# Row sums moved off the early exponentials, and a new stored order, in an attention and gated-MLP kernel

## The chip, the cores and the metric

The kernel runs on one core of a Trainium2 chip. The metric is the device time of one execution in microseconds (us); smaller is better. The engines are TensorE (PE), VectorE (DVE), ScalarE (ACT), GpSimd (POOL) and SyncE (SP), whose queue issues the DMAs.

## The reference

Float32 throughout, with 8 batches of 576 positions, 8 heads of 64.

```
# attention, per batch and head (scale = 1/8)
q_d, k_d, v_d = means over 4 neighbouring positions          # 144 rows
out_up    = repeat(softmax(scale * q_d @ k_d.T) @ v_d, 4)    # pooled half
scores    = scale * q @ k.T, masked to |i - j| < 4
out_local = softmax(scores) @ v                              # local half
x = out_up + out_local                                       # (8, 576, 512)
# MLP with a spatial gate, per batch
h = gelu_tanh(x @ w_in);  u, v = halves of h                 # 512 columns each
v_n = (v - mean(v)) / sqrt(var(v) + 1e-6) * g_ln
v_s = w_sg @ v_n + b_sg
out = x + (u * v_s) @ w_out
```

## The kernel before

The work is cut into small named pieces. A number behind a name is the pair of heads `g` (32 of them: 8 batches of 4 pairs) or, with a dot, batch and tile of the MLP. An order written out by hand in the string `ORDER` says in which sequence the pieces are emitted and, behind a slash, on which engine; each engine runs its own pieces strictly in that sequence. Buffers (8 banks of PSUM `ps`, 10 of `X`, 38 of `R`) are handed out and taken back along the same order.

For one pair: `lq`, `lk`, `lv`, `lw` load q, k and two forms of v; `qs`, `ks`, `vs` sum four neighbours (on POOL two instructions each for q and k). `S` computes the local scores and `Y` the pooled ones (`YS` is both from pair 4 on). `mx`, `nx` and `my`, `ny` take row maxima and biases. `ea` (four) and `eb` (six) are the local exponentials, ten tiles of 64 columns, `ec` the three pooled ones. `re` adds the epsilon to the row sums, `rc` inverts them, `np` and `nq` scale. `T`, `U`, `t` turn the probabilities on PE, `pa`, `pb`, `pc`, `pe` copy them out of PSUM, and `D` multiplies by v. In pairs 0 to 3 `S` adds the mask on PE, and `D` sums v's four neighbours itself: 104 small matmuls. `oe`, `od`, `xa`, `xb` join both halves to x; `xh`, `xl`, `xc` split x into a high and a low part.

For the MLP, `v` (batch 0: `vk` by parts), `u`, `s`, `o` are the four products on PE, three matmuls with 32-bit operands for each product of the split parts. The pieces `w`, `wu`, `wq`, `wb`, `wt`, `wh`, `wl` with a letter `y`, `z` or `r` load a weight matrix and make its two parts; `wq0` to `wq4`, `whq`, `wlq` do so for `w_sg`.

Work that matters for the change: `exp(i)` writes each exponential with `accum_out`, so that ACT also delivers its row sum, which the profile shows as an extra ACTIVATION_READ_ACCUMULATOR. `dma` lets at most six loads be in flight: the seventh waits for the first (`DEPTH`). `lv` of pair g waits for `D` of pair g - 2 while g is below 6. `WARM` puts 28 and 20 matmuls on zeros ahead of `S0` and `S3`, wherever these stand in the order. Loads stand on SP's queue, except four of pairs 0 and 1, which are on ACT's.

Of the kernel before, what the change touches and what calls it, by code (L numbers as in the profile page):

```python
# [90 lines left out]
ea0 lq3 wuy3 qs0/P wly0/P wqy2/A S1 eb0 Y1 mx1 wby2 wuy2 wty3 wty2 Y0 my0 my1 nx1/A ny1/V wqy1/A wby1 ny0/A why3/V ec0
re0/V ec1 rc0 nq0/P wz2 lk3 wqz2/V lq2 S3 ea1 eb1 wbz2 wuz2 lk2 np0/P S2 mx3 ks2/V T0 wz3 wqz3/A qs2/P mx2 re1/A rc1
pa0/A wtz2 U0 lk4 t0 lv0/S qs3/V pb0/A pc0/A nx3/V pe0/V nx2/A lw0/S Y2 my2 ea2 eb2 ny2/A D0 wuy1 ks4/V wbz3 ec2 re2/A
lq4 qs4/V oe0/V od0 np1/P wz1 xa0 xb0 ks3/P nq1/P U1 wty1 rc2 np2/P T1 xh0/V wqz1/A nq2/P lv1/S pa1/V pb1/A pc1/A YS4
ma4 ea3 wz0 mb4 t1 pe1/V lq5 Y3 my3 xl0/P lv2 D1 eb3 wbz1 ny3/A ec3 oe1/A T2 U2 pa2/A pb2/A wqz0/A my4 vk3.0 ny4/A mx4
nx4/A od1 xa1 re3/A wly3/P t2 xb1 small lk5 qs5/P pc2/A rc3 vk1.0 xh1/V ec4 ks5/V lw2 pe2/A D2 nq3/P t3 np3/P why2/A
wbz0 eb4 oe2/V od2 xa2 xb2 T3 pa3/A U3 pb3/V pc3/V pe3/A YS5 my5 lk7 lv3 lw3 D3 wuz0 why1/A wly2/P lk6 ea4 wr0 wr1 ma5
mb5 mx5 xc0 wly1/V xl1/P vk2.0 vk2.1 re4/A rc4 nq4/V t4 ks6/V oe3/V ny5/A ec5 xh2/A xl2/V vk3.1 wuz3 wtz0 whz0/A xc1
wqr0/A nx5/A vk0.0 od3 xa3 xb3 whz2/V vk0.1 xh3/V wlz2/V wur0 wr3 wur3 np4/P xl3/V T4 U4 lv4 wtz3 wuz1 wqr3/A vk1.1
vk1.2 lw4 wq4 wbr0 pa4/A vk2.2 pb4/V wqr1/A wbr1 v0.2 ea5 wbr3 wtz1 ks7/V eb5 vk3.2 lq6 re5/V rc5 vk0.2 v0.0 pc4/A  # L100
pe4/V vs4 whz3/A qs6/V v0.1 vg0.1 v0.3 wtr0 wlz0/V wq2 wlz3/V vb0.1 vk4.0 vk4.1 vg0.2 vg0.0 D4 wur1 YS6 my6 vg0.3 wtr3
whz1/A lq8 vb0.0 xc2 wq0 lv5 vk4.2 nq5/P np5/V ma6 xc3 v0.4 wlz1/V mb6 whq2/A wtr1 ny6/A vb0.2 wq3 u0.3 vp0.0 vn0.0
wlq2/P ec6 vp0.2 mx6 lw5 vp0.1 u0.2 whq3/A wlq3/P va0.4/A vj0.4 wr2 wqr2/A lq7 vh0.0/A vb0.3 vg0.4 ua0.2 ua0.3 u0.4
ua0.4 u0.0 vn0.2 vh0.2/A u0.1 vn0.1 vh0.1/A vb0.4 wq1 whq1/A oe4/A vp0.3 whr3/A T5 vl0.2/V U5 t5 pa5/A u0.7 vn0.3
wlq1/V ua0.0 ua0.1 vl0.0/P vp0.4 u0.6 b vn0.4 vl0.1/V whq0/A wlq0/V whr1/A whq4/A wlq4/V vh0.3/A vl0.3/V vh0.4/A
vl0.4/V ua0.6 nx6/A u0.5 ua0.5 wlr1/V s0.1 sa0.1 wbr2 ea6 sm0.1/P whr0/A s0.3 sa0.3 qs7/V vs5 wlr3/P s0.0 sm0.3/V
sa0.0 sm0.0/V s0.2 eb6 re6/A wur2 wtr2 od4 qs8/V gh0.0/A rc6 nq6/P lk8 pb5/V pc5/V ua0.7 s0.4 sa0.2 np6/P sm0.2/V s0.5
sa0.5 gh0.1/A pe5/A s0.6 xa4 gl0.0/P whr2/A sa0.4 sm0.4/V sm0.5/V gh0.2/A sa0.6 sm0.6/P xb4 s0.7 U6 sa0.7 sm0.7/V
gh0.3/A gl0.3/P T6 pa6/A pb6/A pc6/A D5 oe5/A lw7 gl0.2/V gl0.1/V YS7 my7 od5 ks8/V xa5 xb5 t6 ma7 mb7 pe6/A lk9 lw6
xh4/A lv6 vs6 lq9 o0.7 ny7/A ec7 o0.6 mx7 oa0.6 wlr0/P D6 lv7 YS8 lw8 qs9/V oa0.7 o0.5 nx7/A ea7 lq10 my8 ma8 qs10/V  # L110
mb8 mx8 eb7 xl4/P xh5/V re7/A rc7 ny8/A nq7/V xl5/V wlr2/P o0.0 oe6/A od6 xa6 xb6 lk10 o0.1 ec8 nx8/A eb8 ea8 re8/A
o0.4 ks9/V oa0.4 xc5 t7 np7/P T7 oa0.0 oa0.5 vs7 U7 pa7/A pb7/V pc7/A xc4 rc8 oa0.1 np8/P o0.3 pe7/V D7 oe7/V xh6/A
YS9 lq11 nq8/P od7 xa7 xb7 xh7/A T8 ma9 my9 mb9 mx9 ny9/A ec9 U8 nx9/V ea9 t8 pa8/V pb8/V qs11/V ks10/V xl6/P pc8/A
pe8/V xl7/P os0.0 v1.0 vg1.0 vb1.0 v1.1 vg1.1 lv8 vs8 D8 oe8/A od8 YS10 my10 eb9 xa8 xb8 xc6 lv9 xc7 vb1.1 ma10 re9/V
v1.4 va1.4/A mb10 xh8/A vs9 vp1.1 vn1.1 v1.3 rc9 nq9/V lk12 vg1.3 v1.2 vp1.0 np9/P t9 T9 vj1.4 vn1.0 U9 o0.2 vg1.4 lw9
lk11 vg1.2 ks12/P pa9/A pb9/A pc9/A lq12 ks11/P ny10/A mx10 nx10/A ec10 vb1.3 vp1.3 vn1.3 vh1.3/A vl1.3/P pe9/V
vh1.1/V u1.2 vb1.2 vp1.2 ea10 oa0.2 oa0.3 D9 YS11 vb1.4 my11 vh1.0/V vl1.0/P eb10 ny11/V ma11 mb11 oe9/V re10/A u1.1
rc10 np10/V vl1.1/V nq10/P ec11 u1.4 ua1.4 ua1.2 u1.0 ua1.0 os0.3 vp1.4 ua1.1 mx11 vn1.2 vh1.2/V vl1.2/P T10 pa10/A
vn1.4 lv10 vh1.4/A vl1.4/V vs10 t10 U10 pb10/V u1.3 ua1.3 pc10/V pe10/A lq13 nx11/A ea11 s1.3 qs12/V eb11 xl8/V od9
xa9 s1.0 s1.1 sa1.1 sa1.0 sm1.1/V lk13 re11/A rc11 lw10 D10 YS12 oe10/A lv11 vs11 xb9 sa1.3 xh9/A np11/P sm1.0/P  # L120
nq11/P u1.6 lw11 lq14 qs13/P my12 ny12/A ma12 s1.2 mb12 mx12 ec12 nx12/V ea12 od10 xa10 s1.5 eb12 sa1.2 ua1.6 s1.4
xl9/P T11 xc8 os0.2 pa11/A sm1.3/V sm1.2/P gh1.1/A re12/V rc12 t11 np12/V sa1.5 nq12/P sa1.4 U11 pb11/V pc11/V u1.5
xb10 pe11/A ua1.5 sm1.5/P ks13/V t12 D11 YS13 lv12 oe11/A od11 xa11 lk15 xb11 ma13 T12 pa12/A U12 pb12/A xh10/A s1.6
mb13 pc12/V pe12/A my13 ny13/V ec13 mx13 nx13/V s1.7 lk14 ks14/V u1.7 xl10/V xh11/V xl11/V sm1.4/P v2.0 u2.6 ks15/P
eb13 vs12 qs14/P sa1.6 ea13 re13/V ua2.6 rc13 ua1.7 vg2.0 v2.3 os0.1 np13/P T13 pa13/A gh1.0/V gl1.0/P lw12 sm1.6/V
D12 lv13 oe12/A sa1.7 sm1.7/V gh1.3/V gl1.3/V gl1.1/V YS14 nq13/P U13 od12 xa12 gh1.2/A lw13 t13 vg2.3 vb2.0 xc11 ma14
mb14 gl1.2/P lq15 o1.4 my14 pb13/V xb12 ny14/V vs13 mx14 v2.1 ec14 lq16 o1.0 pc13/V nx14/A vp2.0 vn2.0 vh2.0/V pe13/V
D13 oa1.4 ea14 qs15/V eb14 oa1.0 YS15 my15 re14/V ny15/V ec15 ma15 mb15 mx15 rc14 v2.2 vg2.2 lk16 xc10 xc9 v2.4 lv14
vg2.1 vs14 np14/V vb2.1 T14 lw14 va2.4/A vj2.4 nx15/A nq14/P vl2.0/V oe13/A od13 xa13 xb13 ks16/P vp2.1 qs16/V vn2.1
# [885 lines left out]
```

## Time and profile before

| | us |
|---|---|
| three timed runs | 579.75, 578.34, 578.86 |
| median | 578.86 |
| span of the profiled execution | 578.3 |
| PE busy | 562.3 |
| DVE, ACT, POOL busy | 420.8, 355.8, 309.6 |

The profiled execution has no time of its own beside its span of 578.3 us, from first to last instruction; the timed runs lie 0 to 1.5 above it. A row of the timeline gives start, length, engine, line, operation, out<-in, and in brackets the idle time ahead of it with what ended it. Busy times of an engine overlap with those of others. "PEld" is PE's weight loading, which overlaps its matmuls.

### The profile page before, as it was taken

The page shows a single profiled execution, that of the slowest core. Times are in us where ns is not written, and L with a number is a line of the kernel's source. Part 1 is how long each engine was busy: PE and PEld are TensorE (multiplying, and loading weights), DVE is VectorE, ACT ScalarE, POOL GpSimd, SP SyncE. Part 2 cuts the span into 40 slices and gives each one's busy share as a digit, 9 for nine tenths or more (in the row PEclk, how much of TensorE's full clock was granted, in tenths as well). Part 3 has the DMA queues.
Part 4 walks back from the last instruction along what each step waited for, and adds up shares of the span by engine and source line. Part 5 has one row for each costly group of instructions (what it writes and reads, how often), then busy time and mean ns, then how long its engine had stood idle before and what let it go on. Part 6 is the DMA issues. An engine that isn't in the chain of part 4 may idle for free.

```text
span 578.3 us, 17588 instructions
## 1 busy us (share of the span) xinstructions
PE 562.3 (97%) x7040; PEld 524.0 (91%) x7040; DVE 420.8 (73%) x943; ACT 355.8 (62%) x1239; POOL 309.6 (54%) x391
## 2 busy tenths in 40 slices
...
GB/s 310 276 234 313 98 45 120 96 192 87 140 96 164 24 107 54 208 63 1 86 56 197 114 67 98 41 151 98 87 83 195 103 107 2 18 23 41 43 1 102
DMA packets 30609, 62.73 MB, mean 108 GB/s; under 512 B 3648, under 2 KB 3904, under 8 KB 30528
## 3 DMA queue, kind: packets, MB, share of 16 engines
...
q8 instruction: 55, 0.90, 0.7%
q10 hardware_dynamic: 576, 1.23, 0.6%
q14 instruction: 26, 0.21, 0.1%
...
## 4 chain that ended last, share of the span: by engine, by line
PE 91%; DVE 4%; DMA 2%; ACT 2%; issue 1%; ACTq 0%; DVEq 0%
PE ps L800 55%; PE ps L722 18%; PE ps L604 4%; PE ps L620 3%; PE ps L455 3%; PE ps L543 3%; PE ps L476 3%; PE ps L552 2%; DMA R<-in_qT_dram 1%; PE ps L955 1%; ACT L523 1%; ACT pd L523 1%; DVE stats L485 0%; PE ps L448 0%; DMA R<-in_v_dram 0%
## 5 line engine op out<-in xcount | busy, mean ns | idle before, releaser
L800 PE MATMUL ps<-wsg_h,R 128*128 128x288 f32 x576 | 120.5, 296 | 0.0
L800 PE MATMUL ps<-X,weight_z 128*128 128x288 f32 x512 | 109.4, 297 | 0.0
L800 PE MATMUL ps<-R,weight_r 128*128 128x288 f32 x768 | 108.4, 297 | 1.0 <-ACT R L734 0.8
L800 PEld LDWEIGHTS ps<-R,weight_r 128*128 128x128 f32 x768 | 103.1, 188 | 2.2 <-ACT R L734 0.9
L722 PE MATMUL ps<-weight_y,X 128*128 128x512 f32 x320 | 99.1, 404 | 0.0
L515 ACT ACTIVATE X<-X,nb 128x64 f32<-128x64 f32 x280 | 93.6, 339 | 2.8 <-DVE nb L494 2.3
L800 PEld LDWEIGHTS ps<-wsg_h,R 128*128 128x128 f32 x576 | 94.0, 188 | 0.2 <-DVE R L791 0.2
L800 PE MATMUL ps<-wsg_l,R 128*128 128x288 f32 x320 | 92.5, 295 | 0.0
L800 PEld LDWEIGHTS ps<-X,weight_z 128*128 128x128 f32 x512 | 84.3, 188 | 0.5
L800 PE MATMUL ps<-R,weight_z 128*128 128x288 f32 x256 | 75.5, 295 | 0.0
L722 PEld LDWEIGHTS ps<-weight_y,X 128*128 128x128 f32 x320 | 59.4, 191 | 12.5
L838 DVE SCALAR_TENSOR_TENSOR vs<-ps,g_sb,b_sb 128x288 f32<-128x288 f32 x64 | 32.7, 514 | 49.3 <-PE ps L800 43.9
L232 ACT CAST R<-R 128x512 fp32r<-128x512 f32 (+2 forms) x41 | 26.0, 645 | 62.4 <-DVE R L845 35.2
L800 PEld LDWEIGHTS ps<-wsg_l,R 128*128 128x128 f32 x320 | 60.3, 188 | 0.0
L763 POOL TENSOR_TENSOR rs<-rs,nhalf 128x1 f32<-128x1 f32 (+1 forms) x40 | 25.5, 641 | 64.9 <-DVE rs L754 60.9
L515 ACT ACTIVATION_READ_ACCUMULATOR X<-X,nb 128x1 f32 x280 | 53.5, 191 | 0.0
L722 PE MATMUL ps<-weight_y,R 128*128 128x512 f32 x128 | 51.2, 400 | 0.0
L439 POOL TENSOR_TENSOR pairs<-R 112x256 f32<-112x256 f32 x56 | 44.4, 793 | 9.2 <-DMA R<-in_v_dram 9.2
L845 POOL TENSOR_TENSOR R<-R,vs 128x288 f32<-128x288 f32 x27 | 23.7, 880 | 47.1 <-DVE vs L838 32.0
L800 PEld LDWEIGHTS ps<-R,weight_z 128*128 128x128 f32 x256 | 48.2, 188 | 0.2
L232 ACT COPY R<-ps 112x288 f32<-112x288 f32 (+4 forms) x77 | 30.1, 419 | 27.5 <-PE ps L543 20.0
L791 POOL TENSOR_TENSOR R<-R,R 128x512 fp32r<-128x512 f32 (+1 forms) x22 | 30.6, 1393 | 28.4 <-DVE R L232 6.4
...
## 6 DMA issues: line engine op xcount, KB each, us to landing
...
R<-in_kT_dram SPq DMA_DIRECT2D x31, 293.0 KB, 4.3
...
R<-in_qT_dram SPq DMA_DIRECT2D x30, 293.0 KB, 4.0
weight_y<-in_w_in_dram SPq DMA_DIRECT2D x4, 512.0 KB, 6.0
weight_z<-in_w_in_dram SPq DMA_DIRECT2D x4, 512.0 KB, 6.1
weight_r<-in_w_out_dram SPq DMA_DIRECT2D x4, 512.0 KB, 6.6
```

The lines of the kernel that those rows point to most:

```text
L232: (nc.scalar.copy if e == "A" else ENG[e].tensor_copy)(**kw)
L439: ENG[e].tensor_tensor(out=pairs, in0=v[:, 0:2], in1=v[:, 2:4], op=ALU.add)
L455: nc.tensor.matmul(out=sp[i][os, c * KB:(c + 1) * KB], lhsT=q[hs, t * QB:t * QB + KB], rhs=k[hs, t * QB:t * QB + KB], start=not early, sto ...
L476: nc.tensor.matmul(out=st["sdv"][n][os, cs], lhsT=qd2[par][hs, i * QC:i * QC + HD], rhs=st["kd"][hs, ks], start=True, stop=True)
L515: nc.scalar.activation(out=st["ms"][:, t, :], in_=src, func=AF.Exp, bias=st["nb"][:, t:t + 1], scale=scale, accum_out=sums[par][:, t:t + 1])
L604: nc.tensor.matmul(out=out, lhsT=lhsT, rhs=pdt[ks, probs, h * QC:(h + 1) * QC], start=first, stop=last)
L722: nc.tensor.matmul(out=acc, lhsT=r32(l), rhs=r32(weights[f"y{k}"][:, 0, w]), start=(i == 0 and ks[0] == 0), stop=(i == len(ops) - 1 and ks ...
L763: nc.gpsimd.tensor_tensor(out=rs[0:n], in0=rs[0:n], in1=nhalf[0:n], op=ALU.pow)
L791: ENG[e].tensor_tensor(out=r32(dst), in0=vact[s][0][0:n], in1=vh[0:n, 0:DM], op=ALU.subtract)
L800: nc.tensor.matmul(out=acc[:, 0:HALF], lhsT=r32(l), rhs=r32(r), start=(first and n == 0), stop=(last and n == len(ops) - 1))
L838: nc.vector.scalar_tensor_tensor(out=vsb[i], in0=at["ps", "m", b, "s", i][:, 0:HALF], scalar=g_sb[:, i // 2:i // 2 + 1], in1=b_sb[:, half( ...
L845: ENG[e].tensor_tensor(out=u[:, half(i)], in0=u[:, half(i)], in1=vsb[i], op=ALU.mult)
```

## The change

Three things are changed. First, the local exponentials of the first eight pairs (`SUMMED = 8`) leave out `accum_out`; a new piece `es` on DVE sums the ten tiles in one instruction, and `re` waits for it. Second, the loads of pairs 0 and 1 stand on SP's queue alone. Third, the first 560 pieces of `ORDER`, up to `v1.4`, are in a new sequence, some on another engine; what follows is the same. Line numbers behind the change are 1 to 5 higher.

```diff
 ORDER = """
-lk0/A ks0/P wy0 wqy0/V lk1/S ks1/P wby0 lq0/A wy3 S0 mx0 nx0/V lq1/A wuy0 wqy3/V wy2 wty0 wy1 why0/V wby3 lw1/A qs1/P
+lk1 ks1/V lq1 S1 lq0 qs0/V qs1/V Y1 mx1 nx1/V lk0 ks0/P wy0 wuy0 wqy0/V wy2 lk2 ea1 eb1 wby0 wty0 lq2 wuy2 why0/A Y0
...
+SUMMED = 8
...
-        early, early_d = g < EARLY_S, g < EARLY_D
+        early, early_d, summed = g < EARLY_S, g < EARLY_D, g < SUMMED
...
                     nc.scalar.activation(out=st["ms"][:, t, :], in_=src, func=AF.Exp, bias=st["nb"][:, t:t + 1],
-                                         scale=scale, accum_out=sums[par][:, t:t + 1])
+                                         scale=scale, accum_out=None if summed else sums[par][:, t:t + 1])
...
+        def row_sums(e):
+            nc.vector.tensor_reduce(out=sums[par][:, 0:NT], in_=st["ms"], axis=AX.X, op=ALU.add)
...
-        dq = {"S": 0.5, "A": 0.5} if g < 2 else {"S": 0.5}
-        dq2 = {"S": 1.0, "A": 1.0} if g < 2 else {"S": 1.0}
+        dq, dq2 = {"S": 0.5}, {"S": 1.0}
...
-        add(N("re"), {"A": 0.2, "V": 0.17}, total, [N("ea"), N("eb"), N("ec")])
+        if summed:
+            add(N("es"), {"V": 0.75}, row_sums, [N("ea"), N("eb"), N("rc", 2)])
+        add(N("re"), {"A": 0.2, "V": 0.17}, total, [N("es") if summed else None, N("ea"), N("eb"), N("ec")])
```

The first place is the start of PE's program. Before, the 28 matmuls on `zeros` came first, and these rows are the last of them and the start of `S0` (L448 adds the mask, L455 are the scores):

```order
55 L955 LDWEIGHTS zeros
56 L955 MATMUL ps_170<-zeros 128x256
57 L448 MATMUL ps_199<-mask_sb,ident_sb 128x256
58 L448 MATMUL ps_200<-mask_sb,ident_sb 128x384
59 L455 MATMUL ps_199<-R_149,R_166 64x64 x2
```

Now PE starts with `S1` (rows 1 to 10), then `Y1` and `Y0` (11 to 22, L477), and the matmuls on `zeros` follow, ahead of `S0`:

```order
1 L449 MATMUL ps_154<-mask_sb,ident_sb 128x256
2 L449 MATMUL ps_155<-mask_sb,ident_sb 128x384
3 L456 MATMUL ps_154<-R_149,R_152 64x64 x2
4 L456 MATMUL ps_155<-R_149,R_152 64x64 x2
...
11 L477 MATMUL ps_182<-kd_89,qd_81 64x144 x2
12 L477 MATMUL ps_183<-kd_89,qd_81 64x144 x2
...
17 L477 MATMUL ps_229<-kd_88,qd_80 64x144 x2
18 L477 MATMUL ps_230<-kd_88,qd_80 64x144 x2
...
23 L960 LDWEIGHTS zeros
24 L960 MATMUL ps_244<-zeros 128x256
```

`S1`, `Y1` and `Y0` moved ahead of the 28 matmuls, and `S0`, which was the first to use PE, behind them.

The second place is the start of ACT's work behind its first load of a function table. Before, ACT went from the first weight piece `wuy0` to the exponentials of pair 0 (`nb_95` is its bias); a load of v stood between:

```order
5 L346 ACTIVATE weight_y_154<-weight_y_154 128x512
6 L224 DMA X_241<-in_vw_dram 128x640
7 L515 ACTIVATE X_246,sums_86<-ps_199,nb_95 128x64 x4
8 L346 ACTIVATE weight_y_168<-weight_y_168 128x512
9 L334 ACTIVATE weight_y_230<-weight_y_230 128x512
10 L515 ACTIVATE X_246,sums_86<-ps_200,nb_95 128x64 x6
```

Now the exponentials of pair 1 come first, and those of pair 0 (row 14) stand behind seven other pieces and behind `nx0`, the bias of pair 0 (row 11); `sums` is no longer among the outputs of L516:

```order
3 L516 ACTIVATE X_208<-ps_154,nb_96 128x64 x4
4 L516 ACTIVATE X_208<-ps_155,nb_96 128x64 x6
5 L347 ACTIVATE weight_y_204<-weight_y_204 128x512
6 L233 CAST weight_y_227<-R_220 128x512
7 L233 CAST wsg_h<-R_297 128x576
8 L505 ACTIVATE nbd_98<-stats_85 128x3
9 L524 ACTIVATE pd_93,sums_87<-ps_182,nbd_98 128x3x48 x2
10 L524 ACTIVATE pd_93,sums_87<-ps_183,nbd_98 128x3x48
11 L493 ACTIVATE nb_95<-stats_84 128x10
12 L532 ACTIVATE sums_87<-sums_87 128x13
13 L505 ACTIVATE nbd_97<-stats_84 128x3
14 L516 ACTIVATE X_357<-ps_273,nb_95 128x64 x4
```

Pair 0 moved behind pair 1, with the copies of two weights (L233) between, and the loads left this queue.

The third place is PE between `D2` and `YS5`, which `D3` follows. Before, `t3` (L552), `T3` (L543) and `U3` stood there:

```order
269 L620 MATMUL ps_805<-R_760,X_801 64x58 x2
270 L552 MATMUL ps_859<-turn_p,pd_93 112x112 x2
271 L543 MATMUL ps_880<-turn_l,X_647 128x122 x4
272 L543 MATMUL ps_887<-turn_l,X_647 128x122
273 L552 MATMUL ps_887<-turn_p,pd_93 112x112 x3
274 L476 MATMUL ps_896<-kd_89,qd_81 64x144 x2
275 L476 MATMUL ps_897<-kd_89,qd_81 64x144 x2
```

Now `T3` and `U3` stand ahead of `D2`, and after `t3` (L556) come the three matmuls of `vk2.0` (L727):

```order
268 L624 MATMUL ps_802<-R_641,X_626 64x58 x2
269 L556 MATMUL ps_868<-turn_p,pd_93 112x112 x2
270 L727 MATMUL ps_886<-weight_y_227,X_772 128x512 x2
271 L727 MATMUL ps_886<-weight_y_227,R_799 128x512
272 L477 MATMUL ps_907<-kd_89,qd_81 64x144 x2
273 L477 MATMUL ps_908<-kd_89,qd_81 64x144 x2
```

Two turns moved ahead of `D2`; `vk3.0` and `vk1.0`, which stood ahead of it, are behind `D3`, and `vk2.0` is between.

More of the change, by code (lines that the diff above doesn't have):

```diff
@@ L89 @@
 ORDER = """
-lk0/A ks0/P wy0 wqy0/V lk1/S ks1/P wby0 lq0/A wy3 S0 mx0 nx0/V lq1/A wuy0 wqy3/V wy2 wty0 wy1 why0/V wby3 lw1/A qs1/P
[L91 to L129, printed above, removed]
@@ L130 @@
-vh2.1/A pa14/A lq17 U14 pb14/V t14 vg2.4 pc14/A pe14/A o1.5 u2.0 oa1.5 os1.2 ua2.0 u2.4 ua2.4 vb2.2 vp2.2 vn2.2
-vh2.2/V xh13/A o1.2 ea15 D14 vb2.4 oe14/A vl2.2/P eb15 vp2.4 re15/A YS16 ma16 u2.1 oa1.2 mb16 o1.6 mx16 nx16/V o1.7
-lq18 o1.3 eb16 lk18 vb2.3 my16 vl2.1/P ny16/V vn2.4 vh2.4/A oa1.6 xh12/A ec16 vp2.3 vn2.3 vh2.3/V vl2.3/V vl2.4/P
+lk1 ks1/V lq1 S1 lq0 qs0/V qs1/V Y1 mx1 nx1/V lk0 ks0/P wy0 wuy0 wqy0/V wy2 lk2 ea1 eb1 wby0 wty0 lq2 wuy2 why0/A Y0
+qs2/P my1 S0 wq1 whq1/A wqy2/V wby2 wty2 lq3 wy1 S2 wz2 es1 ny1/A ec1 wlq1/P mx0 my0 nx0/A qs3/P ks2/V re1/A rc1 np1/P
@@ new lines @@
+mx2 ny0/A ea0 eb0 es0 lk3 ec0 wqy1/A re0/V rc0 nx2/A np0/V wby1 S3 nq0/P wqz2/A Y2 nq1/P U0 lv0 why2/A wuy1 wty1 wy3
+ks3/P mx3 my2 lk4 wly0/P ea2 T0 pa0/V eb2 pb0/A pc0/A lw1 ny2/A t0 es2 nx3/V lw0 wly2/V pe0/A D0 lk5 ec2 re2/A Y3 rc2
+why1/A wbz2 ea3 eb3 oe0/A lq4 np2/P qs4/P lq5 ks4/V wuy3 T1 pa1/A U1 t1 lv1 pb1/A pc1/A wz0 lw2 T2 pe1/A od0 my3 ny3/A
+xa0 nq2/P pa2/A es3 qs5/V xb0 lv2 ec3 re3/A wqy3/A rc3 wuz2 YS4 my4 U2 t2 ny4/A ec4 pb2/A pc2/V D1 ma4 wly1/P np3/P T3
+mb4 xh0/A nq3/P U3 oe1/A wqz0/A wr3 lv3 wby3 wtz2 wty3 pe2/A lw3 xl0/P D2 wz1 mx4 pa3/A whz2/A ks5/V pb3/A pc3/A
```

36 lines of the change are left out of this document (added).

## The prediction

> **What bounds the kernel.** I read the page first, then the busy times by stage, TensorE's (PE's) timeline, the DMA queues by window, and ScalarE's (ACT's) timeline. The page:
>
> ```profile
> span 578.3 us, 17588 instructions
> ...
> PE 562.3 (97%) x7040; PEld 524.0 (91%) x7040; DVE 420.8 (73%) x943; ACT 355.8 (62%) x1239; POOL 309.6 (54%) x391
> ...
> q8 instruction: 55, 0.90, 0.7%
> ...
> PE 91%; DVE 4%; DMA 2%; ACT 2%; issue 1%; ACTq 0%; DVEq 0%
> ```
>
> PE is the bound: 16.0 us of the span are idle, and no order can gain more than these and what a slow clock costs. So the question is where PE is not at work in the part that the change re-sorts. The two orders are the same from v1.4 on, which PE reaches at 126.9. By stage (columns: stretch, length, busy time and count of PE, weight loads, DVE, ACT, POOL, then granted clock, DMA share, GB/s):
>
> ```profile
> 6.10:10.20 4.10, 3.36 (x48) 2.12 (x48) 3.13 (x7) 0.70 (x1) 3.54 (x6) 1.00 1.03 400
> ...
> 0.00:8.10 8.10, 6.23 (x32) 4.20 (x33) 4.63 (x25) 1.99 (x2) 3.14 (x13) 1.00 0.72 254
> 8.10:24.80 16.70, 14.63 (x250) 10.74 (x250) 14.56 (x32) 13.03 (x65) 13.26 (x16) 0.90 0.87 303
> 24.80:43.30 18.50, 16.26 (x484) 14.14 (x480) 17.01 (x40) 18.12 (x94) 15.22 (x17) 1.00 0.82 255
> 43.30:50.80 7.50, 3.01 (x120) 2.76 (x108) 4.21 (x10) 7.30 (x25) 4.37 (x5) 0.87 1.02 310
> 50.80:56.10 5.30, 5.30 (x15) 4.12 (x16) 5.27 (x9) 0.00 (x0) 3.65 (x5) 0.53 1.02 316
> 56.10:126.90 70.80, 70.41 (x964) 65.77 (x962) 62.96 (x130) 58.24 (x188) 46.48 (x54) 1.00 0.38 120
> ```
>
> After 56.1 PE lacks 0.39 us; all that can be won lies ahead of it: 10.7 us idle, 4.49 of them in 43.3 to 50.8, and a clock of 0.53 just behind. The timeline of PE:
>
> ```profile
> 1.05 4.92 PE L955 MATMUL ps<-zeros 128*128 128x256 bf16 x28 [1.05 <-DVE zeros L279]
> 6.08 1.31 PE L448 MATMUL ps<-mask_sb,ident_sb 128*128 128x256 f32 x4
> 8.13 0.93 PE L455 MATMUL ps<-R,R 64*64 64x64 f32 x40 [0.74 <-DMA R<-in_qT_dram]
> ...
> 39.64 0.79 PE L620 MATMUL ps<-R,X 64*64 64x58 f32 x34
> ...
> 42.27 0.53 PE L476 MATMUL ps<-kd,qd 64*64 64x144 f32 x11 [0.69 <-DVE R L627]
> ...
> 45.00 0.56 PE L620 MATMUL ps<-R,X 64*64 64x58 f32 x20
> 50.06 0.69 PE L620 MATMUL ps<-R,X 64*64 64x58 f32 x14 [4.49 <-issue]
> 50.67 1.22 PE L722 MATMUL ps<-weight_y,X 128*128 128x512 f32 x2
> 51.70 0.63 PE L722 MATMUL ps<-weight_y,R 128*128 128x512 f32 x1
> ...
> 59.71 0.62 PE L722 MATMUL ps<-weight_y,X 128*128 128x512 f32 x2
> 60.17 0.40 PE L722 MATMUL ps<-weight_y,R 128*128 128x512 f32 x1
> ```
>
> The long wait stands in the middle of D3, between matmuls that read the same tiles, and its releaser is "issue": no operand was late. I read it as PE's own code. The page has 14,080 matmuls and weight loads and 55 packets of queue q8: 256 instructions a packet. The DMA rows of two windows, 42.7 to 47.2 and 47.2 to 50.1 (queue: packets, MB, share of the 16 engines):
>
> ```profile
> q1 hardware_dynamic: 769, 1.47, 98.0%
> ...
> q1 hardware_dynamic: 380, 0.76, 101.4%
> q8 instruction: 1, 0.02, 2.6%
> ```
>
> In the first, data alone moved, at 98% of the engines; in the second came one packet of code, and PE went on at 50.06. YS5 and D3 are 160 matmuls, 320 instructions, that PE eats in 4.0 us (42.27 to 45.56, and the 0.69), faster than a packet gets through a full data queue. [...]
>
> The clock fell behind that wait: a group of three matmuls took 1.45 us at 50.67 (until 52.12) and 0.70 at 59.71. That is worth 0.47 of the 5.3 us at 0.53, some 2.5 us. So D3 costs about 7.0 us altogether, the largest sum in reach.
>
> **The change, part by part.** *Exponentials without accumulators.* ACT's timeline:
>
> ```profile
> 6.11 0.70 ACT L346 ACTIVATE weight_y<-weight_y 128x512 int32<-128x512 uint32 x1 [2.68 <-DMA weight_y<-in_w_in_dram]
> ...
> 10.22 0.32 ACT L515 ACTIVATE X<-ps,nb 128x64 f32<-128x64 f32 x1 [3.42 <-DVE nb L494]
> 10.43 0.19 ACT L515 ACTIVATION_READ_ACCUMULATOR X<-ps,nb 128x1 f32 x1
> 10.53 0.31 ACT L515 ACTIVATE X<-ps,nb 128x64 f32<-128x64 f32 x1
> ...
> 38.54 0.36 ACT L232 COPY R<-ps 112x192 f32<-112x192 f32 x1
> ```
>
> Each readout puts the next exponential 0.10 us later (10.43 to 10.53). Eighty go, 8.0 us, of which 40 (4.0 us) ahead of D3. Bounds for the 40: 0, if an exponential alone keeps the 0.31 spacing, and 7.6, if the whole 0.19 goes; I take 4.0, since the starts show it. Eight row sums come to DVE, and two more table loads to ACT (56 in the order, 54 before), the extra ones behind D3. Nearest rows, from the groups of instructions:
>
> ```profile
> L487 DVE TENSOR_REDUCE stats<-X 128x10 f32<-128x640 f32 x6 | 4.9, 818 | 0.1
> ...
> L346 ACT ACT_TABLE_LOAD x1 | 1.3, 1283 | 2.1 <-issue 2.1
> ```
>
> The sums read the same 128x640: 0.82 each, 6.5 us in all, and each stands between the exponentials and the reciprocal that T and U wait for. So a pair's chain loses 1.0 and gains 0.8: nothing, within bounds of -1.1 and +0.8 (readout's two ends). Both hide behind PE from D4 on, where PE lacks 0.39 us in 70.8; without that cover the two table loads are 2.6 us.
>
> *The warm-up.* The 28 matmuls on zeros are tied to S0, and S0 is no longer first. They ran from 1.05 to 5.97, while PE had no data; now they stand behind S1, Y1 and Y0. The first five loads on the one queue are k1, q1, q0, k0, wy0. Sizes and landing, and the POOL sums of k0:
>
> ```profile
> R<-in_kT_dram SPq DMA_DIRECT2D x31, 293.0 KB, 4.3
> ...
> weight_y<-in_w_in_dram SPq DMA_DIRECT2D x4, 512.0 KB, 6.0
> ...
> out_dram<-R SPq DMA_DIRECT2D x2, 144.0 KB, 1.8
> ```
>
> ```profile
> 6.42 0.67 POOL L425 TENSOR_TENSOR half<-R 128x288 f32<-128x288 f32 x1 [4.00 <-DMA R<-in_kT_dram]
> 7.17 0.43 POOL L426 TENSOR_TENSOR kd<-half 128x144 f32<-128x144 f32 x1
> ```
>
> At 254 GB/s 2.06 MB had moved by 8.1, so 1.2 MB by 6.0, counting back at the 400 GB/s of 6.1 to 10.2; k0 ends 1.2 MB, wy0 1.72 MB. With 1.3 us from the last byte to the release (144 KB take 1.8, of them 0.5 moving) k0 lands at 7.3 and wy0 at 8.6. ACT's first use of a weight thus goes from 6.11 to 8.6 (+2.5; bounds +1, as the ramp of one queue is not in the trace, and +4). k0's sums end at 8.4, Y0 at 9.3, the warm-up at 14.2, S0 (1.31 + 0.93) at 16.4. Before, S0 ended at 9.06. ACT's first exponential followed that by 1.16 (10.22); now the bias of pair 0 comes at 17.6. ACT, whose queue stands behind it, is through with pair 1 at about 15.0 (8.6, ten exponentials at 0.21, wuy0, wuy2, why0 and whq1 at 0.7, and 1.3 for ny1 and ec1, an estimate of four times 0.31): a wait of 2.6, plus 0.2 ahead of pair 1, where 3.42 stood.
>
> *ACT up to pe2, the last evacuation for D2* (38.54 above). The order puts 13 pieces more ahead of it (nx0, ny1, oe0, pa1, pe0, pe1, whq1, why0, why1, why2, wqy3, wqz2, xh0: 6.7 us) and takes 7 away (nx1, nx4, pa0, pc2, wqy2, wqz1, wqz3: 3.5 us). These rows price the weight pieces at 0.7; the small ones are 0.2 to 0.55, the 0.36 above among them:
>
> ```profile
> L334 ACT ACTIVATE weight_z<-weight_z 128x512 f32<-128x512 f32 x3 | 2.1, 701 | 0.0
> ...
> L232 ACT CAST weight_y<-R 128x512 fp32r<-128x512 f32 x2 | 1.3, 672 | 0.0
> ```
>
> The end of pe2: 38.90 + 2.5 - 0.6 + 3.2 - 4.0 = 40.0, 1.1 later. D2 ended 1.53 behind it (40.43) and does so again, at 41.5. Then come t3 (0.36), vk2.0 (0.72) and YS5, at 42.6 where it began at 42.27: +0.3.
>
> *Work left.* Before, vk3.0 and vk1.0 were done by D3; now only vk2.0 is: +0.7 behind it, where PE is full.
>
> *Code.* D2 to D3 lose T3, U3 and the wait of 0.69 between them: three blocks of code in a row with little pause. At 40 to 46 the queue now holds wz1, wr0, wr2 and wz3 at 512 KB, as it held wr0, wr1, wr3. I let the wait in D3 and its clock stand, and add 1.0 for the block ahead of it (bounds 0, and 2.4 if that fetch too is as slow as the one in D3).
>
> *DVE, POOL and SP.* DVE has 37 pieces ahead of the third reciprocal, 47 before, so the four sums (3.3 us) find room; POOL has 17 ahead of np3, 23 before. SP's loads of v for pairs 2 and 3 wait for D0 and D1 as before, with smaller loads behind them: nothing, up to +1 where D1 is late.
>
> **Sum.** 0.3 + 0.7 + 1.0 = +2.0 on the span of 578.3: 580.3. The median of the runs, 578.86, lies 0.56 above that span, so 580.9. About 0.3% (1.7 us) is what a measurement here can tell from none.
>
> **Rivals.** *The wait in D3 shrinks (faster).* One mechanism: the code for D3 finds a gap in the data queue, because v for pair 3 is held back by D1. It decides once D3's wait is below about 3 us. Left at 1.5 us it gives back 3.0, and a clock that stays up 2.5 more: 580.9 - 5.5 = 575.4. For it: PE entered its earlier blocks without such a wait, and the 0.69 before YS5 is put to DVE. Against: 512 KB loads crowd the same stretch. [...]
>
> *Even.* The wait loses 2 us and the clock still falls: 578.9. The same comes out if the change does less than it says, readouts and row sums cancelling and the later start being absorbed in the wait. Whether a wait of 2.5 us costs the clock too, no row shows. [...]
>
> *New waits behind D3.* D6 stands one u piece behind T6, and its evacuation pe6 is on DVE behind five others (1.0, an estimate of two of the 0.36 copies and their neighbour); with 1.3 us for each extra table load in front of PE: 580.9 + 3.6 = 584.5. Against: 0.39 us of idle PE in 70.8.
>
> **Chances.** The forecast, 579.8 to 583 on its own, 0.40; D3's wait shrinks 0.22, of which 0.03 by the rule of hidden code; the clock spared 0.05; even 0.23; new waits 0.10. From these: faster by over 0.3% 0.27, within 0.3% 0.29 (even, and 0.06 of the forecast's low end), slower 0.44. The range 575.0 to 584.0 leaves about 0.1 out on each side.
>
> **What would show it.** PE's first warm-up matmul near 9 us; S0 ending near 16.4 and an ACT wait of some 2.6 us for its bias; no readouts at the exponentials of the first eight pairs; D2 ending near 41.5; one or two waits on "issue" between D2 and the end of D3, summing to over 4 us, no q8 packet in them until the end, and a clock below 1 behind. The prediction is wrong if D3 runs through with under 2 us of wait, or if PE idles after D4 by more than 1 us.

## The result and the profile after

The changed kernel takes 583.61 us (median of four runs, 582.16 to 585.93), beside 578.95 us of the kernel before on the same chip (578.34 to 579.75): ratio 1.0079, 95% interval 1.0055 to 1.0104. It is slower by 4.7 us; the forecast said 2.0, with 579.8 to 583 as its own stretch and 575.0 to 584.0 as the whole range.

A profile is one execution, and executions differ. The first profile of before has a span of 578.3 us. The same kernel, profiled a second time for this study, has 576.9 and a time of 578.65 us, 1.79 above its span, as all its timed runs are. So the first one (about 580.0) lay above the median, and the second stands for the usual run; below, "before" with two numbers gives both. The page after, its lines on span and busy time:

```profile
span 581.9 us, 17493 instructions
PE 561.7 (97%) x7040; PEld 523.5 (90%) x7040; DVE 420.4 (72%) x930; ACT 354.5 (61%) x1176; POOL 316.6 (54%) x396
```

PE is as busy as before (562.3); the span is longer by idle time. PE's waits after (us in total, times, longest):

```profile
PE ps L449 <- DVE mask_sb L294: 4.6, 1, 4.6
PE ps L624 <- issue: 3.9, 1, 3.9
PE ps L805 <- ACT R L233: 1.2, 1, 1.2
...
PE ps L805 <- DVE R L796: 1.2, 1, 1.2
...
PE ps L805 <- DVE R L862: 0.6, 1, 0.6
```

The first is the start: the 28 matmuls on zeros no longer fill it. The second is D3's wait (L620 before, L624 now). The other three stand behind D3, where before had almost none; the rows left out stand ahead of D3, or behind v1.4 as in before. Busy times by stretch (length, then PE, PEld, DVE, ACT, POOL, granted clock, DMA share, GB/s), after:

```profile
24.80:43.30 18.50, 16.16 (x489) 13.99 (x493) 15.04 (x33) 17.25 (x68) 15.30 (x15) 1.00 0.78 234
43.30:58.30 15.00, 11.11 (x127) 9.15 (x120) 9.54 (x20) 10.47 (x34) 8.62 (x12) 0.77 0.96 304
58.30:126.90 68.60, 65.61 (x872) 60.52 (x874) 63.05 (x120) 57.21 (x163) 54.01 (x62) 1.00 0.33 100
```

The same three stretches of before, second profile:

```profile
24.80:43.30 18.50, 16.61 (x505) 14.80 (x509) 17.01 (x41) 18.00 (x92) 15.12 (x17) 1.00 0.78 235
43.30:58.30 15.00, 11.55 (x119) 9.46 (x110) 12.64 (x21) 9.45 (x34) 8.98 (x8) 0.77 1.03 299
58.30:126.90 68.60, 67.79 (x948) 63.55 (x947) 61.27 (x129) 57.01 (x181) 45.08 (x53) 1.00 0.36 115
```

From 58.3 to 126.9 PE now idles 2.99 us, where it idled 0.81 (0.39 in the first profile), while DVE went to 63.05 of 68.60 and POOL from 45.08 to 54.01. The clock around D3 is the same. The places of PE's pieces, read off its timeline, tell how the difference adds up:

| us | before, 1st | before, 2nd | after |
|---|---|---|---|
| D2 ends | 40.43 | 39.43 | 39.50 |
| D3 ends | 50.74 | 48.71 | 49.61 |
| v1.4 starts | 126.86 | 125.08 | 129.91 |
| span | 578.3 | 576.9 | 581.9 |

Against the usual run 0.9 us are lost by D3's end and 3.9 from there to v1.4; what follows adds 0.2. Of the 3.9, 0.7 is the work left (only vk2.0 was done). Three pieces that ran through in before now take longer by 3.8 us with the waits in them: u0.0 by 1.5, s0.0 by 1.5, o0.4 by 0.85, against 0.8 of waits in before's second profile. Those terms give 3.7 of the 3.9. (PE's idle time alone grew by 2.2 us; each of the three pieces grew by 0.2 to 0.3 us more than the wait in it.)

Each of the three is an evacuation (a copy out of PSUM) or a low part that its own engine reaches late. For u0.0 it is pa5, which frees T5's bank of PSUM. ACT, after:

```profile
70.24 2.50 ACT L516 ACTIVATE X<-X,nb 128x64 f32<-128x64 f32 x10
72.64 0.97 ACT L233 COPY R<-ps 128x464 f32<-128x464 f32 x3
```

and PE there, after:

```profile
68.89 0.27 PE L547 MATMUL ps<-turn_l,X 122*128 122x122 f32 x1
...
73.22 0.40 PE L805 MATMUL ps<-X,weight_z 128*128 128x288 f32 x1 [1.24 <-ACT R L233]
```

The turns are done by 69.2 and the copies start at 72.64, behind ten exponentials. For s0.0 it is vl0.4 on DVE, behind ma8, mb8, od6 and vl0.3. DVE, after:

```profile
88.58 0.87 DVE L464 TENSOR_TENSOR X<-ps,mask_sb 128x256 f32<-128x256 f32 x2
89.38 0.44 DVE L595 SCALAR_TENSOR_TENSOR od<-ps,da 128x288 f32<-128x288 f32 x1
89.74 2.43 DVE L796 TENSOR_TENSOR R<-R,R 128x512 fp32r<-128x512 f32 x2
```

For o0.4 it is gl0.2 on DVE (L862). In before, the MLP's products stood further ahead of the attention pairs: T5 came behind u0.0 and D5 behind s0.0, now both come ahead of them (T5 at 66.8 and not 76.1, D5 at 76.6 and not 97.7, first profile), and their side work stands on ACT and DVE ahead of what u0.0, s0.0 and o0.4 need.

### The profile page after: what moved, and what is told of

Read it like the earlier page. It is cut to its first block, busy times and chain, and to the rows that moved or that the text cites. A ratio compares the mean times of both kernels' runs of the same rounds, so it can differ in the third digit from the quotient of the medians.

```text
span 581.9 us, 17493 instructions
## 1 busy us (share of the span) xinstructions
PE 561.7 (97%) x7040; PEld 523.5 (90%) x7040; DVE 420.4 (72%) x930; ACT 354.5 (61%) x1176; POOL 316.6 (54%) x396
## 4 chain that ended last, share of the span: by engine, by line
PE 75%; DVE 9%; ACT 7%; DMA 6%; issue 2%; POOL 0%; SPq 0%; ACTq 0%
PE ps L805 49%; PE ps L727 14%; PE ps L608 2%; PE ps L547 2%; PE ps L624 2%; DMA weight_y<-in_w_in_dram 2%; PE ps L556 2%; PE ps L456 2%; PE ps L477 2%; ACT X L516 2%; DMA weight_z<-in_w_in_dram 1%; DMA R<-in_qT_dram 1%; ACT pd L524 1%; ACT L524 1%; DMA R<-in_v_dram 1%
## 5 line engine op out<-in xcount | busy, mean ns | idle before, releaser
L805 PE MATMUL ps<-X,weight_z 128*128 128x288 f32 x512 | 110.6, 298 | 1.2 <-ACT R L233 1.2
L727 PE MATMUL ps<-weight_y,X 128*128 128x512 f32 x320 | 98.2, 403 | 0.0
L516 ACT ACTIVATE X<-X,nb 128x64 f32<-128x64 f32 x280 | 90.2, 337 | 2.2 <-DVE nb L495 1.8
L727 PEld LDWEIGHTS ps<-weight_y,X 128*128 128x128 f32 x320 | 59.4, 192 | 12.3
L233 ACT CAST R<-R 128x512 fp32r<-128x512 f32 (+2 forms) x40 | 25.3, 642 | 57.6 <-DVE R L850 32.2
L768 POOL TENSOR_TENSOR rs<-rs,nhalf 128x1 f32<-128x1 f32 (+1 forms) x40 | 24.2, 607 | 63.0 <-DVE rs L759 61.2
L727 PE MATMUL ps<-weight_y,R 128*128 128x512 f32 x128 | 51.3, 401 | 0.7 <-POOL R L643 0.7
L796 POOL TENSOR_TENSOR R<-R,R 128x512 fp32r<-128x512 f32 (+1 forms) x24 | 33.1, 1380 | 34.3 <-ACT R L233 9.3
L850 POOL TENSOR_TENSOR R<-R,vs 128x288 f32<-128x288 f32 x29 | 26.3, 909 | 40.9 <-DVE vs L843 26.4
L805 PEld LDWEIGHTS ps<-R,weight_z 128*128 128x128 f32 x256 | 48.2, 188 | 0.2
L233 ACT COPY R<-ps 128x116 f32<-128x116 f32 (+4 forms) x83 | 30.9, 414 | 27.8 <-PE ps L547 11.2
L516 ACT ACTIVATION_READ_ACCUMULATOR X<-X,nb 128x1 f32 x240 | 45.3, 189 | 0.0
```

The lines of the kernel that those rows point to most:

```text
L233: (nc.scalar.copy if e == "A" else ENG[e].tensor_copy)(**kw)
L516: nc.scalar.activation(out=st["ms"][:, t, :], in_=src, func=AF.Exp, bias=st["nb"][:, t:t + 1], scale=scale, accum_out=None if summed else ...
L727: nc.tensor.matmul(out=acc, lhsT=r32(l), rhs=r32(weights[f"y{k}"][:, 0, w]), start=(i == 0 and ks[0] == 0), stop=(i == len(ops) - 1 and ks ...
L768: nc.gpsimd.tensor_tensor(out=rs[0:n], in0=rs[0:n], in1=nhalf[0:n], op=ALU.pow)
L796: ENG[e].tensor_tensor(out=r32(dst), in0=vact[s][0][0:n], in1=vh[0:n, 0:DM], op=ALU.subtract)
L805: nc.tensor.matmul(out=acc[:, 0:HALF], lhsT=r32(l), rhs=r32(r), start=(first and n == 0), stop=(last and n == len(ops) - 1))
```

## The experiments

All ratios are to the kernel before, run on the same chip in the same session. The changed kernel was not run again in the later sessions, so its variants are compared with it by these ratios.

| what | median us | ratio, 95% |
|---|---|---|
| the change | 583.61 | 1.0079 (1.0055 to 1.0104) |
| new order and queue, accumulators kept | 588.92 | 1.0176 (1.0153 to 1.0199) |
| before, sums on DVE | 583.77 | 1.0100 (1.0079 to 1.0122) |
| before, one queue | 577.94 | 0.9980 (0.9962 to 0.9997) |
| the change, warm-up first | 585.48 | 1.0113 (1.0092 to 1.0133) |
| the change, three waits moved | 586.21 | 1.0145 (1.0125 to 1.0164) |
| the same, with followers | 585.31 | 1.0103 (1.0076 to 1.0131) |
| before, short D3 | 578.57 | 0.9987 (0.9972 to 1.0003) |
| the change, short D3 | 581.63 | 1.0052 (1.0036 to 1.0069) |
| before, vk ahead of D3 | 579.47 | 0.9999 (0.9983 to 1.0016) |
| before, two loads later | 578.70 | 0.9993 (0.9977 to 1.0010) |
| before, two loads later, one queue | 577.72 | 0.9982 (0.9962 to 1.0002) |

**The kernel before again.** No edit.

> The kernel before itself, profiled a second time, to see how much of a difference between two profiles is the run and not the kernel. Theory H (the windows at half clock come and go from run to run, and the first profile had one more than the usual run): span 576 to 577.5, with 1.7 us less of half clock, and the waits of PE as in the first profile within 0.5 us. Rival: D3's wait itself varies, and is 3 us or less in this run; then the smaller wait in the kernel with the two loads moved says less than it seems to.

Span 576.9, time 578.65. PE's waits:

```profile
PE ps L620 <- issue: 3.5, 1, 3.5
```

The span and the slow stretch near 15 us (below), now absent, are as theory H said. But D3's wait was 3.5 and not 4.5: there neither the theory (waits within 0.5) nor the rival (3 or less) holds as it was put. The long wait varies by a microsecond from run to run, so a profile alone does not show a gain of that size there.

**The parts of the change.** The order and the queue without the new sums:

```diff
-SUMMED = 8
+SUMMED = 0
```

with es0 to es7 taken out of the order.

> The changed kernel with the accumulators back: SUMMED = 0 and the pieces es0 to es7 taken out; new order and single queue stay. Theory A (the order makes the loss): as slow as the changed kernel, 583.0 to 585.0, since the readouts put 0.1 us onto each of 80 exponentials on ACT and the same evacuations stand behind them. Rival C (the row sums on DVE make the loss): 579 to 580.5.

It is 5.3 us slower than the change, more than theory A allowed, and rival C is wrong: in this order the sums on DVE are worth about 1% of the time. Two rows of PE's waits, one behind D3 and one ahead of it:

```profile
PE ps L805 <- ACT R L233: 2.2, 1, 2.2
PE ps L608 <- ACT R L233: 1.8, 1, 1.8
```

Most is lost early, in ACT's queue and by the clock that follows. The second row is D0, which waits for copies on ACT and starts at 27.39 (25.01 in the change); right behind it PE runs at half clock, from 27.61 to 31.02 (0.91 in the mean of 24.8 to 43.3). D0 ends 4.0 us later than in the change (31.48 against 27.45), D3 4.4 us (54.01 against 49.61). Behind D3 the wait of u0.0 for pa5 grew from 1.2 to 2.2, because the ten exponentials ahead of pa5, with readouts, take 3.33 us from the first start to pa5's (74.14 to 77.47) and not 2.40 (70.24 to 72.64 above), but the idle time from 58.3 to 126.9 is nearly the same, 3.3 us against 3.0. Three windows at half clock, where the change has two (mean clock 0.991 and 0.994), stand at D0, behind D3 and behind the wait of u0.0.

The sums alone, in the old order, each right ahead of `re`:

```diff
-mx2 re1/A rc1
+mx2 es1 re1/A rc1
```

and so for the other seven, with `SUMMED = 8`.

> The kernel before with the exponentials of the first eight pairs without accumulators and the eight row sums on DVE, each right ahead of re; order and queues otherwise as before. Theory A: the readout saves about 1.0 us for a pair on ACT and the sum gives back 0.8 on DVE, both beside PE: 578.0 to 579.7. Rival C (row sums make the loss): 582 or more.

Theory A missed by 4 us and more, and the time is the one that rival C named. DVE of this kernel:

```profile
22.84 0.89 DVE L486 TENSOR_REDUCE stats<-ps 128x4 f32<-128x256 f32 x2 [0.28 <-PE ps L456]
23.64 0.81 DVE L528 TENSOR_REDUCE sums<-X 128x10 f32<-128x640 f32 x1
```

and its ACT:

```profile
24.49 0.21 ACT L532 ACTIVATE sums<-sums 128x13 f32<-128x13 f32 x1 [3.58 <-DVE sums L528]
```

The row sum costs its 0.81 and, far more, its place: the exponentials of pair 1 were done by 19.8, but es1 stood on DVE behind two row maxima, the sums of k and weight pieces, and started at 23.64. So re1 on ACT waited 3.58 us and all evacuations behind it; in before's second profile re1 ran at 21.9. YS4 and YS5 came late, and the half clock lasted 10.2 us at D3 (this profile has a mean clock of 0.984, the timed runs a median of 0.991). DVE has little room there: 14.56 of 16.70 us busy from 8.1 to 24.8 in before's first profile, 17.01 of 18.50 behind. So this run does not price the sum; it prices a sum put into a full queue.

The queue alone:

```diff
-lk0/A lq0/A lq1/A lw1/A
+lk0 lq0 lq1 lw1
```

> The kernel before with its four loads of pairs 0 and 1 that stood on ACT's queue (lk0, lq0, lq1, lw1) on SP's queue; nothing else. Theory A: the start shifts by less than 1 us and is caught up in the waits up to D3: 578.3 to 580.0. Rival B (the single queue makes the loss): 581.5 or more.

The single queue is worth -0.2%, and its interval just keeps clear of 1: no loss comes from it. The warm-up put back to the start:

```diff
-WARM = {"S0": 28, "S3": 20}
+WARM = {"S1": 28, "S3": 20}
```

> The changed kernel with the 28 matmuls on zeros tied to S1, the first use of PE, as they were tied to the first use before (WARM S1 and S3). Theory A (the loss is behind D3): S0 ends some 3 us earlier, at 12.5, and D0 by 1 us at most, since D0 waits for evacuations on ScalarE; D3's wait takes what is left: 582.4 to 583.8. Rival B (the later warm-up makes the loss): 581 or less.

It is no faster than the change (the intervals of the two overlap), so rival B is wrong; the median is above what theory A allowed, so A has not the whole of it. D2 ends at 39.52, where the change has 39.50: the start is hidden. Two of its PE waits:

```profile
PE ps L624 <- issue: 5.5, 1, 5.5
...
PE ps L805 <- ACT R L233: 1.2, 1, 1.2
PE ps L805 <- DVE R L796: 1.2, 1, 1.2
```

D3's wait came out at 5.5 here, and u0.0 and s0.0 wait as long as in the change although PE reaches them 2 us later. That fits a chain within the stretch: ACT and DVE get their work from PE's own earlier products, so an earlier or later PE meets the same wait. The change with the short D3, below, has the same 1.2 and 1.2 with PE 1.5 us earlier.

**The waits behind D3.** First try, three groups moved ahead:

```diff
-U5 od4 nx6/A ea6 ... t5 wlz1/P pa5/A xa4 pb5/A pc5/A
+U5 pa5/A pb5/A pc5/A od4 nx6/A ea6 ... t5 wlz1/P xa4
-vn0.3 YS8 lk9 ma8 mb8 od6 vh0.3/A vl0.3/V ea7 u0.7 b vl0.4/V vl0.2/P s0.0
+vn0.3 vh0.3/A vl0.3/V vl0.4/V vl0.2/P YS8 lk9 ma8 mb8 od6 ea7 u0.7 b s0.0
-sm0.7/P gh0.3/V wlr1/V v1.0 vg1.0 gl0.2/V gl0.3/P
+gl0.2/V sm0.7/P gh0.3/V wlr1/V v1.0 vg1.0 gl0.3/P
```

> The changed kernel with three groups of pieces moved, each to a place just ahead of where PE waited for it: pa5, pb5, pc5 right behind U5 (u0.0 waited 1.2 us for a PSUM bank that pa5 had to free), vh0.3, vl0.3, vl0.4, vl0.2 ahead of YS8 (s0.0 waited 1.2 us for vl0.4), gl0.2 right behind gl0.1 (o0.4 waited 0.6 us for the gl pieces). Theory A (the loss is new PE waits behind D3, made by the places of these pieces): the three waits go, 583.6 - 3.0 = 580.6, range 579.9 to 581.6. Rival B (the loss comes from the start: the later warm-up and the single queue) and rival C (the row sums load DVE and delay everything): the waits move to the next piece in line, and the time stays at 582.5 or more.

Theory A fell in this form: the waits moved on, as its rivals had said, and the time rose to 586.21. (What the rivals gave as the cause is ruled out by the runs above.) PE's waits:

```profile
PE ps L805 <- DVE X L464: 2.7, 1, 2.7
...
PE ps L608 <- ACT R L739: 1.2, 1, 1.2
```

u0.0 ran through, and D5 waited instead; vl0.4 came first, and s0.0 waited 2.7 for ma8, which now stood behind it. Second try, with the followers moved as well:

```diff
+U5 pa5/A pb5/A pc5/A od4 ... t5 pe5/A wlz1/P
+vh0.4/A vl0.4/P lw7 vn0.2 vh0.2/A vl0.2/P wlq3/V vn0.3 YS8 lk9 ma8 mb8 vh0.3/A wqr1/A vl0.3/V od6 ea7
+gl0.0/V wlr1/V gh0.2/A gh0.1/A gl0.1/V gl0.2/V
```

> The changed kernel with the three waits behind D3 taken away again, with their followers: pa5, pb5, pc5 behind U5 and pe5 right behind t5 (pe5 is what D5 waited for in the first try); vl0.4 and vl0.2 both on POOL, each right behind its vh, and od6 and wqr1 behind what s0.0 waits for; gl0.2 and wlr1 ahead of gl0.3. Theory A (single pieces stand in the wrong place): waits at u0.0, D5, s0.0 and o0.4 sum to under 0.8 us where they were 3.0, no new one over 0.5: 583.5 - 2.5 = 581.0, range 580 to 582. Theory F (ScalarE and VectorE together are behind in this stretch, whatever piece waits): the waits turn up at other pieces again, and the time is 583 or more.

What theory F foretold came: all three waits are smaller or gone, and others have come. PE's waits, and the stretch behind D3:

```profile
PE ps L805 <- ACT R L824: 1.0, 1, 1.0
PE ps L477 <- ACT R L824: 1.0, 1, 1.0
PE ps L805 <- DVE X L464: 0.7, 1, 0.7
```

```profile
58.30:126.90 68.60, 64.65 (x822) 59.32 (x821) 57.70 (x117) 55.69 (x155) 52.12 (x59) 1.00 0.32 99
```

PE idles 3.95 us of it, where the change has 2.99. So in neither try were three misplaced pieces the loss behind D3: whichever piece went ahead, another was late. That ACT and DVE owe more at once in this order fits both tries, but it is argued; neither engine is full over the whole stretch (DVE 57.70 and ACT 55.69 of 68.60 us). What order would clear it stays open.

**D3's wait.** It is the largest single wait in both kernels behind the start. That its "issue" is PE's code can be counted: before's first profile and after together have three waits of PE on "issue" of over 0.3 us. D3's, 4.49 and 3.89, stand behind 1,729 of PE's instructions (matmuls, weight loads and semaphore instructions) in both, with 14 of D3's matmuls left in before and 8 in after; the third, 0.39 at L455 in before, stands behind 3,009. The places lie 1,280 apart, five packets of 256. Three kinds of edit tried to take the wait away. First a D3 with little code:

```diff
-EARLY_S, EARLY_D = 4, 4
+EARLY_S, EARLY_D = 4, 3
...
-YS5 my5 lk7 lv3 lw3 D3
+YS5 my5 lk7 lv3 lw3 vs3 D3
```

> The kernel before with EARLY_D = 3: v of pair 3 is summed over four neighbours on POOL (a new piece vs3 ahead of D3), so D3 is 8 matmuls with long operands and not 104 small ones. Theory D (D3 waits for its code, since PE eats 256 small instructions faster than one packet of code gets through a full data queue): the wait of 4.5 us falls below 1, the clock stays up behind it (2.8 us of half clock go), D3 has about 0.8 us less work: 578.4 - 3.7 - 2.6 - 0.8 = 571.3, range 570 to 574. Rival E (D3 waits for something that is late anyway, such as a load): the wait stands in another row and the time is 576.5 or more.

The wait in D3 is gone and the clock holds, as the theory said; the time hardly moves. PE's waits and its stretches from 43.3:

```profile
PE ps L604 <- DVE R L232: 1.7, 2, 0.9
PE ps L455 <- issue: 1.5, 2, 1.3
PE ps L722 <- DVE R L639: 1.3, 1, 1.3
```

```profile
43.30:58.30 15.00, 13.19 (x144) 10.05 (x144) 14.02 (x23) 12.60 (x44) 12.14 (x11) 1.00 1.03 327
58.30:126.90 68.60, 66.79 (x943) 62.44 (x942) 62.30 (x133) 55.47 (x178) 46.58 (x55) 1.00 0.33 99
```

D3 ends at 45.10, 3.6 us ahead of before's second profile, though another wait on code, of 1.3 us, came up in YS5. By v1.4 1.8 are left (123.25 against 125.08), and 1.4 of the span (575.5 against 576.9): PE meets new waits, above all the one of 1.3 for a low part of x on DVE (L639). Of the half clock 2.65 us were saved in the profile (half of the 1.88 and 3.41 that PE was busy in the second profile's two windows at 0.50). The timed runs show 0.5 (not measurable from none), though their mean clock is higher too (median 0.997, before 0.994); where the rest went in the usual run, no profile shows.

> The changed kernel with the same edit, EARLY_D = 3 and vs3 ahead of D3. Theory D: its wait of 3.9 us in D3 and 2.5 us of half clock go with 0.8 us of work, and the waits behind D3 (3.0 us) stand: 583.4 - 3.2 - 2.3 - 0.8 = 577.1, range 575.5 to 580. Theory F (ScalarE and VectorE are the bound behind D3 in the new order, so that PE, being earlier, waits for them longer): half of it comes back as longer waits at u0.0, s0.0, o0.4, 579.5 to 582.

The same edit in the changed kernel gives 581.6, in the interval of theory F, though not by its mechanism: a wait on code of 2.1 us moved into YS5, the clock still fell (0.994 in the mean, 1.000 in before with the short D3), and the waits at u0.0 and s0.0 kept their 1.2 each:

```profile
PE ps L456 <- issue: 2.1, 1, 2.1
...
PE ps L805 <- ACT R L233: 1.2, 1, 1.2
...
PE ps L805 <- DVE R L796: 1.2, 1, 1.2
```

Then more work for PE in front of the wait, without a change of code:

```diff
-my4 vk3.0 ny4/A ... rc3 vk1.0 xh1/V ... lv3 lw3 D3
+my4 ny4/A ... rc3 xh1/V ... lv3 lw3 vk3.0 vk1.0 D3
```

> The kernel before with vk3.0 and vk1.0 moved from ahead of D2 to between YS5 and D3: 1.5 us of slow matmuls in the block of code whose successor is late. Theory D: the wait in D3 shrinks by about 1.4 us to 3.0, and if that keeps PE busy for over half of the clock's window, the slow stretch shrinks by one window of 3.4 us (1.7 us): 578.4 - 1.4 = 577.0, or 575.3 with the window; range 575 to 578. Rival E: 578.4 or more, the wait keeps its end.

Even, as rival E had it, though the wait did shrink. The waits show why:

```profile
PE ps L620 <- issue: 2.7, 1, 2.7
PE ps L604 <- ACT R L232: 1.3, 1, 1.3
```

D3's wait shrank to 2.7, as expected against the first profile, and D2, which vk3.0 and vk1.0 had covered, now waits 1.3 us for its evacuations: moved cover is not new cover.

Then less data ahead of the code:

```diff
-lk6 ea4 wr0 wr1 ma5 ... wur0 wr3 wur3 np4/P ... wuz1 wqr3/A vk1.1
+lk6 ea4 wr0 ma5 ... wur0 np4/P ... wuz1 vk1.1
-vk1.2 lw4 wq4 wbr0 pa4/A
+vk1.2 lw4 wq4 wr1 wr3 wbr0 wur3 wqr3/A pa4/A
```

> The kernel before with two loads of 512 KB, wr1 and wr3, issued behind wq4 and not ahead of lv4 (they were 1 MB of what stood in the data queue when D3's code was asked for), and the two pieces wur3 and wqr3 that use wr3 moved later on ScalarE, into its idle stretch. Theory D (the code's packet stands behind data in the queue): at some 300 GB/s the packet comes 3 us sooner, D3's wait falls from 4.5 to 1.5 us or less and the clock loses one window of 3.4 us less or none: 579.0 - 3.0 - 1.7 = 574.3, and 1 us of that comes back as waits for x behind D3: 575.3, range 573.5 to 577. Rival G (the packet comes some 4.5 us after it is asked for, whatever the queue holds): the wait stands, 578 or more.

In its profile the packet came 2.1 us after its block was entered (the block ahead, that is: 256 instructions before the wait), and D3's wait was 1.8:

```profile
47.08 0.45 PE L620 MATMUL ps<-R,X 64*64 64x58 f32 x14 [1.75 <-issue]
```

The timed runs are even, though, and the same edit with the single queue shows the old wait again:

> The kernel before with two edits that each measured a little faster or even alone: the four loads of pairs 0 and 1 on SP's queue, and wr1, wr3 issued behind wq4 with wur3, wqr3 later on ScalarE. If the two add up: 0.998 x 0.9993 of the kernel before, 577.6, range 576.5 to 578.5. If the packet in D3 again comes 2 us and not 4.5 after it is asked for and PE keeps what it wins there: 575.5.

PE of that kernel, and the DMA rows of 41.2 to 45.7 and of 45.7 to 48.2 in it (its block was entered at 41.24):

```profile
48.18 0.70 PE L620 MATMUL ps<-R,X 64*64 64x58 f32 x14 [4.13 <-issue]
```

```profile
q1 hardware_dynamic: 630, 1.24, 99.4%
...
q1 hardware_dynamic: 476, 0.93, 101.5%
q8 instruction: 1, 0.02, 2.6%
```

Without wr1 and wr3 ahead of it the queue is as full, 99%, and the packet 4.5 us late: the next loads move up. So D3's wait ends 2.4 to 2.8 us after the start of a packet of code that shares the engines with a nearly full data queue (88 to 107% of them), in both profiles of before (packet at 47.27, PE at 50.06; 45.59 and 48.02), in after (46.63 and 49.12) and in these two (44.59 and 47.08; 45.76 and 48.18); two loads less do not empty that queue, and 1.8 us was one run. In before's first profile the blocks that PE entered at 65.87 and 93.50, with no data moving until the packet came, got it after 0.83 and 0.22 us, those entered at 27.13 and 37.95, with 106 and 90% of the engines busy, after 2.74 and 2.10. Not every block fits that: 1.56 us with 7% (entered at 32.64), 1.10 with 91% (116.16). Why it takes 4.56 at D3 stays open. Fewer loads in flight (`DEPTH`) was not tried. This last kernel is, with the single queue alone, the fastest measured, 0.9982 and 0.9980; only the second interval keeps clear of 1.

## Why the prediction was right in its direction and wrong in its mechanism

*The start (+0.3).* PE's warm-up began at 10.05 (near 9 was said) and S0 ended at 15.54 (16.4). The ACT wait of 2.6 us for nx0 was 1.1:

```profile
16.26 0.21 ACT L493 ACTIVATE nb<-stats 128x10 f32<-128x10 f32 x1 [1.12 <-DVE stats L486]
```

pe2 ended at 37.1, not at 40.0. That term is the one that failed early on: it added a late start and 3.2 us of pieces to ACT as if ACT had been full all along; of the 3.42 us that ACT waited for pair 0's bias before, 1.12 are left, and the exponentials are shorter:

```profile
9.51 2.13 ACT L516 ACTIVATE X<-ps,nb 128x64 f32<-128x64 f32 x10
```

D2 ended 0.1 us off before's second profile, 2 earlier than foretold; YS5 began at 41.43.

*The readouts.* 0.93 us for ten exponentials (3.33 and 2.40), 3.7 for the 40 ahead of D3, near the 4.0 taken. That the sums find room on DVE was right in this order, 15.04 of 18.50 us from 24.8 to 43.3. "Nothing" for the exchange against the sums was wrong: without it this order is 5.3 us slower, and in the old order it costs 5.3. The exchange is priced by the queues around it; against the bounds of -1.1 and +0.8 for a pair's chain, the whole kernel moved by 5.3 us either way.

*The code (+1.0 and the wait that stands).* D3's wait stood, at 3.89, with the packet of code only in its later part and the clock at 0.50 from 47.25 to 54.08, as foretold. DMA rows of 42.1 to 46.6 and 46.6 to 49.2, after:

```profile
q1 hardware_dynamic: 749, 1.44, 88.4%
...
q1 hardware_dynamic: 461, 0.92, 103.0%
q8 instruction: 1, 0.02, 2.4%
```

The extra wait ahead of D3 did not come; the 0.69 before YS5 is put to xl0 on POOL. The term was 1.0 too large. *The work left (+0.7)* was right.

So the forecast's own terms, 2.0 in all, measured 1.6 (0.9 by D3's end and 0.7 of work left), though not each by itself. That they come so near is luck: the 0.9 is against before's second profile, and half of it is D3's wait, which differs by 1.0 between the two profiles of before; against the first, from which the forecast was worked out, D3 ends 1.1 us earlier. The sum missed 2.7 us, which lies in the rival "new waits behind D3", with its chance of 0.10 and its 3.6 us: the three pieces took 3.0 us longer, net of before's waits. It named the wrong pieces, pe6 and the two table loads; the rows name pa5, vl0.4 and gl0.2. The step that failed is "Both hide behind PE from D4 on, where PE lacks 0.39 us in 70.8": PE lacks 2.99 us there now, and by the prediction's own sign ("if PE idles after D4 by more than 1 us") it is wrong. A stretch that is full in the old order says nothing of the new, in which the MLP's cover stands elsewhere; the string `ORDER` shows where: T5 ahead of u0.0, D5 ahead of s0.0, and pa5 behind ten exponentials. The measured 583.61 lies above the forecast's own 579.8 to 583; that it is still inside the whole range is luck as far as the sum goes.

*The clock.* The prediction left open whether a wait of 2.5 us costs the clock, and gave a spared clock a chance of 0.05, for which no run shows a reason: every profile with a wait on "issue" of 1.75 us or more has a mean clock of 0.984 to 0.997. The clock fell behind 2.7 us in one piece (vk ahead of D3: the two matmuls behind it took 1.22 us, as in before at 50.67, and 0.62 in before at 59.71), and in before's first profile with no wait above 1.2 (busy 1.61 of 3.41 us from 11.37 to 14.78, then 0.50; the prediction's own row of 0.90 from 8.10 to 24.80). With 1.75 (two loads later) the mean clock was 0.994, with the short D3 in before, where no wait on code was over 1.3, 1.000. What went ahead of the slow windows is in the last section.

*A D3 that runs through.* Its chance was 0.03, and no run shows a reason for it: every profile with 104 small matmuls in D3 has a wait on "issue" in it or in YS5, of 1.75 us (two loads later) to 5.5 (the change, warm-up first).
